# How q is turned for batches 1 to 7, and how a build-time planner chooses its next operation

## The chip, the cores and the metric

The kernel runs on one core of a Trainium2 chip, all of it in float32. The metric is the device time of one execution in microseconds, shown as the median of three runs. A profile is one execution recorded by the hardware profiler. The engines are called as in the profile: PE (TensorE), with PEld for its weight loads, DVE (VectorE), ACT (ScalarE), POOL (GpSimd) and SP (SyncE, which issues most DMAs here).

## The reference, cut to what matters

```python
# q, k, v: (8 batches, 8 heads, 576 rows, 64); w1: (4, 512, 1024); w2: (4, 1024, 512)
kv = np.einsum('bhsd,bhse->bhde', k, v)
out = np.einsum('bhsd,bhde->bhse', q, kv)
rms = np.sqrt(np.mean(out * out, axis=-1, keepdims=True) + 1e-06)
attn = out / rms * g_norm
x = attn.transpose(0, 2, 1, 3).reshape(4608, 512)
p = domain_probs / (domain_probs.sum(-1, keepdims=True) + 1e-09)
for e in range(4):
    h = np.maximum(x @ w1[e], 0.0)
    out_moe += p[:, e:e + 1] * (h @ w2[e])
```

A linear attention without softmax, each head's row scaled by the root of its mean square, and then four experts whose outputs are summed with weights.

## The kernel before

**Work and steps.** The 4608 rows of x are cut into nine chunks of 512: chunk b (0 to 7) holds 512 rows of batch b, and chunk 8 the 64 rows that each batch leaves over. There are 36 steps, s = 9e + c, each one expert e on one chunk c. A step has an `up` part (x @ w1, ReLU) and a `down` part (h @ w2); both replace some products by sums of blocks (seven products in place of eight, in two layers: `up`, `down_deep`; one layer in `down`). Step 0 is plain in `up_plain`. Attention for chunk c + 1 is done inside step c of expert 0, so steps 0 to 6 carry the attention of batches 1 to 7. Batch 0 is done ahead of all, in `opening`.

**The planner.** The order is not that of the code. Each piece of work is entered in a `Plan` as an operation with a key (its wanted place, in steps), a cost for each engine that may do it, the buffers it reads and writes, and further predecessors (`after`). `Plan.layout` (L91) then plays the operations through at build time and writes down one order for every engine; an engine may take an operation at most `REACH` keys beyond its first waiting one (L53). Buffers come from pools: `big`, `small`, `xf`, `q`, `kv` and others in SBUF, and eight PSUM banks in four kinds, two each: `u1` and `u2` (for `up`), `db` (for `down`), `ab` (for attention and some of `down_deep`). On the chip every engine goes through its list strictly in order, and waits by semaphores.

Three marks steer the choice: `early` keeps spare buffers free ahead of time, `gang` (on `attend`) reserves the banks of an operation that needs several at once, and `opens` holds back an operation that would take such a bank. In `down`, a list `firsts` and the list `second` add `after` edges between the first products of its two halves.

**Attention of batches 1 to 7** (`attention`, L888), for two groups s of two head pairs each:
- q's 576 rows of four heads arrive in 16 DMAs a batch, in runs of 32 numbers, so that halves of q's 64 dimensions lie on blocks of 32 partitions; DVE's transpose of 32 x 32 blocks (L975) then turns q in place.
- `key_values` (L996, matmuls at L1001): forty 64-column matmuls sum k'v for the two pairs into one `ab` bank; ACT copies the result.
- `attend` (L1021): 32 matmuls for the 512 rows into two `ab` banks (L1028), and 4 for the remaining 64 rows into two `db` banks (L1037).
- `evacuate` (L906): ACT or DVE copies the four results to SBUF, over q's own buffer.
- `norm_rows` (L914): ACT squares (L927), DVE sums (L933), POOL raises to the power -1/2 (L940, L944), DVE multiplies (L950).
- `turn_x` (L1066, L1069): eight 128 x 128 transposes on PE into two `ab` banks, and ACT writes them as chunk b's x with the gain (L1078).
- once a batch, `turn_left` (L1088): two transposes for the remainder, stored to a DRAM tile `x_left` (L1104).

**Attention of batch 0** (`opening`, L677) has another path: q's rows are loaded whole, PE turns q in `turn` (L742), ACT copies it; `attend` (L788) handles one pair at a time; `scaled` (L625) squares from PSUM (L640), sums (L647), raises to the power (L654, L658), and multiplies straight from PSUM (L667); `turn_x` (L806) does four transposes; the 64 remaining rows go through `turn_rem` (L832), `attend_rem` (L850), and `turn_xrem` (L866).

All products of the experts, and only they, run through the helper `halves_of` (L406, the matmuls at L410): each 128-column product is two matmuls of 64 columns.

Of the kernel before, what the change touches and what calls it, by code (L numbers as in the profile page):

```python
# [25 lines left out]
class Op:  # L26
    def __init__(self, key, cost, fn, reads, writes, kb, port):
        self.key, self.cost, self.fn, self.kb, self.port = key, cost, fn, kb, port
        self.outs = list(writes)
        self.bufs = list(dict.fromkeys(list(reads) + self.outs))  # L30
        self.deps = {}
        self.start = self.end = self.eng = None
        self.marks = self.seed = None
        self.early = self.gang = self.opens = False


BANKED = ("u1", "u2", "db", "ab")


class Plan:  # L40
# [12 lines left out]
    REACH = {"PE": 1.1, "DVE": 0.9, "ACT": 0.9, "POOL": 0.9, "SP": 1.0}  # L53
# [10 lines left out]
    def add(self, key, cost, fn, reads=(), writes=(), parts=(), kb=0, after=(), port=False, holds=(),  # L64
            early=False, gang=False):
# [3 lines left out]
        op.early, op.gang = early, gang  # L69
# [21 lines left out]
    def layout(self, slots, later, idle, idle_banks, idle_until):  # L91
# [60 lines left out]
        t = 0.0  # L152
# [4 lines left out]
        def ready(op, eng):  # L157
# [10 lines left out]
            for k, n in need.items():  # L168
                spare = self.SPARE.get(k, 0) if k != "xf" or op.key < self.FORMS else 0
                ahead = op.key > front + 0.1 and (eng == "SP" or op.early)  # L170
                if len(free[k]) < n + (spare if ahead else 0):
                    return None
# [11 lines left out]
        while left:  # L184
# [4 lines left out]
            for eng in todo:  # L189
# [9 lines left out]
                kept = {}  # L199
                for op in pending:  # L200
# [6 lines left out]
                    if op.opens and any(b.kind in kept for b in op.outs):  # L207
                        continue
                    when = ready(op, eng)
                    if when is None:  # L210
                        if op.gang and all(d.start is not None and d.end < t for d in op.deps):
                            kept.update((b.kind, True) for b in op.outs if b.kind in BANKED)
                        continue
                    if when > t:
                        if op.gang and all(d.end < t for d in op.deps):
                            kept.update((b.kind, True) for b in op.outs if b.kind in BANKED)
                        heapq.heappush(wake, when)
                        continue
# [77 lines left out]
def kernel(  # L296
# [76 lines left out]
    for kind, n in BANKS.items():  # L373
# [8 lines left out]
    QW = S * D // 32  # L382
    small_home = pool.tile([P, 4 * 2 * NT], F32, tag="small", name="small")
    kv_flat = kv_home[:].rearrange("p n x -> p (n x)")
    slots["kv"] = [kv_flat[:, i * KV:(i + 1) * KV] for i in range(4)]
    slots["kvbd"] = [kv_flat[:, 4 * KV + i * P:4 * KV + (i + 1) * P] for i in range(4)]
    slots["q"] = [small_home[:, i * QW:(i + 1) * QW] for i in range(2)]
    slots["small"] = [small_home[:, 2 * QW + i * NT:2 * QW + (i + 1) * NT] for i in range(3)]
# [3 lines left out]
        (("small", "q"), "w2y", [small_home[:, 2 * i * NT:2 * (i + 1) * NT] for i in range(2)]),  # L392
        (("small", "q"), "big", [small_home[:, 2 * i * NT:2 * (i + 1) * NT] for i in range(2, 4)]),
# [52 lines left out]
    def norm_probs(key):  # L446
        by_batch = moe_domain_probs.rearrange("(b s) e -> s b e", s=S)

        def load_all(eng):
            nc.sync.dma_start(  # L450
                out=p_all[:, 0:NR, :],
                in_=moe_domain_probs[0:NT, :].rearrange("(p r) e -> p r e", r=NR),
            )
            for r in range(NR):
                nc.sync.dma_start(  # L455
                    out=p_all[:, NR + r:B * NR:NR, :], in_=by_batch[r * P:(r + 1) * P, 1:, :])
# [15 lines left out]
        plan.add(key, {"SP": 4.0}, load_all, writes=[probs], kb=72)  # L472
# [204 lines left out]
    def opening(key, span, rem):  # L677

        b = 0
# [9 lines left out]
        splits = ((96, 6, 0),)  # L689

        def load_pair(hp):
            hs = slice(2 * hp, 2 * hp + 2)
            n = f"{b}_{hp}"
            kt, vt, qt = Buf("big", f"k{n}"), Buf("big", f"v{n}"), Buf("big", f"q{n}")
            want = key - 1 + 0.1 * hp
            load(
                want, qt, lambda qt=qt: qt.ap[:, 0:NT].rearrange("p (h x) -> p h x", h=2),
                q[b, hs, 0:NT, :].rearrange("h (p r) d -> p h (r d)", r=NR), 172,
            )
            for t, src in ((kt, k), (vt, v)):  # L700
                at_ = 0
                for rows, n_, size in splits:
                    load(
# [4 lines left out]
                        241,  # L708
# [15 lines left out]
        groups = ((0,), (1,), (2,), (3,))  # L724
        for g, pairs in enumerate(groups):
# [4 lines left out]
            for o, hp in enumerate(pairs):  # L730
# [4 lines left out]
                qT = qTs[hp] = Buf("big", f"qT{b}_{hp}")  # L735

                def turn(eng, bank=bank, qt=qt):
                    for r in range(NR):
                        rs = slice(r * P, (r + 1) * P)
                        for o in range(2):  # L740
# [7 lines left out]
                    at(hp), {"PE": 0.82}, turn, reads=[qt], writes=[bank])  # L748
# [3 lines left out]
                        out=qT.ap[:, 0:NT], in_=bank.ap[:], func=ACT.Copy),  # L752
# [3 lines left out]
            def key_values(eng, bank=kbank, held=held):  # L756
# [12 lines left out]
                at(pairs[-1]), {"PE": 0.73 * size + 0.2}, key_values,  # L769
# [8 lines left out]
            kind = ("db", "u2", "u1", "db")[g]  # L778
# [21 lines left out]
            for o, hp in enumerate(pairs):  # L800
                bank = Buf("ab", f"xT{b}_{hp}")

                def turn_x(eng, bank=bank, x=x, o=o):
# [13 lines left out]
                    reads=[bank, gains], parts=[xh],  # L817
# [4 lines left out]
        qr = Buf("big", f"qr{b}")  # L822
        load(
            at(1), qr, lambda: qr.ap[0:REM, 0:NT].rearrange("p (h d) -> p h d", d=D),
# [3 lines left out]
        qTr = Buf("big", f"qT{n}")  # L828
# [14 lines left out]
        rawr = [Buf("db", f"raw{n}_{r}") for r in range(2)]  # L843
# [16 lines left out]
        xr = Buf("big", f"x{n}")  # L860
# [3 lines left out]
        def turn_xrem(eng):  # L864
            for cc in range(NPAIR):
# [12 lines left out]
            reads=[xb], writes=[xs],  # L878
        )
        plan.add(  # L880
            at(NPAIR + 1) + 0.1, SPC,
            lambda eng: nc.sync.dma_start(
                out=x_left[:, :, b * REM:(b + 1) * REM],
                in_=xs.ap[:].rearrange("p (k t) -> p k t", k=4)),
            reads=[xs], writes=[left[b]], kb=128,
        )

    def attention(b, key, span, rem):  # L888

        at = lambda j: key + span * j / (NPAIR + 1)  # L890
        R = 32
        G = P // R
        splits = ((120, 4, 0), (96, 1, 480))

        def rows_of(t):

            at_ = 0
            for rows, n_, _ in splits:
                for j in range(n_):
                    yield [  # L900
                        t.ap[0:rows, at_ + (h * n_ + j) * D:at_ + (h * n_ + j + 1) * D]
                        for h in range(2)
                    ]
                at_ += 2 * n_ * D

        def evacuate(key, bank, src, to, dst, n):  # L906
            plan.add(
                key, {"ACT": 0.155 + 0.00088 * n, "DVE": 0.155 + 0.00104 * n},
                lambda eng: nc.vector.tensor_copy(out=dst(), in_=src()) if eng == "DVE"
                else nc.scalar.activation(out=dst(), in_=src(), func=ACT.Copy),  # L910
                reads=[bank], parts=[to],
            )

        def norm_rows(key, name, x, squares, count):  # L914

            ss, rt = Buf("ss", f"ss{name}"), Buf("rt", f"rt{name}")
            width = count * D

            def by_head(ap):
                return ap.rearrange("p (b d) -> p b d", d=D)  # L920

            for at_ in range(0, width, NT):
                n = min(width, NT)
                sq = squares or Buf("ab", f"sq{name}_{at_}")
                plan.add(
                    key, act(n),
                    lambda eng, sq=sq, at_=at_, n=n: nc.scalar.activation(  # L927
                        out=sq.ap[:, 0:n], in_=x.ap[:, at_:at_ + n], func=ACT.Square),
                    reads=[x], writes=[sq],
                )  # L930
                plan.add(
                    key, dve(n),
                    lambda eng, sq=sq, at_=at_, n=n: nc.vector.reduce_sum(  # L933
                        out=ss.ap[:, at_ // D:(at_ + n) // D], in_=by_head(sq.ap[:, 0:n]),
                        axis=AX.X),
                    reads=[sq], parts=[ss],
                )

            def power(eng):
                nc.gpsimd.tensor_scalar(  # L940
                    out=ss.ap[:, 0:count], in0=ss.ap[:, 0:count], scalar1=1.0 / D, scalar2=EPS,
                    op0=ALU.mult, op1=ALU.add,
                )
                nc.gpsimd.tensor_tensor(  # L944
                    out=rt.ap[:, 0:count], in0=ss.ap[:, 0:count], in1=mhalf[:, 0:count], op=ALU.pow)

            plan.add(key - 0.3, {"POOL": 0.3 + 0.19 * count}, power, reads=[ss], writes=[ss, rt])
            plan.add(
                key, dve(width),
                lambda eng: nc.vector.tensor_tensor(  # L950
                    out=by_head(x.ap[:, 0:width]), in0=by_head(x.ap[:, 0:width]),
                    in1=rt.ap[:, 0:count].unsqueeze(2).to_broadcast([P, count, D]), op=ALU.mult,
                ),
                reads=[x, rt], writes=[x], port=True,
            )

        xr, xs = Buf("snap", f"x{b}_r"), Buf("snap", f"xs{b}")
        for s in range(2):
            n = f"{b}_{s}"
            when = at(2 * s)  # L960
            qt = Buf("q", f"q{n}")
# [801 lines left out]
```

## Time and profile before

| what | us |
|---|---|
| median of 3 runs (lowest, highest) | 1665.1 (1664.63, 1666.04) |
| the profiled execution's own time | 1666.04 |
| its span, first to last instruction | 1664.0 |
| DVE busy | 1250.9 |
| ACT busy | 972.7 |
| POOL busy | 705.1 |

The span lies inside the time of its own execution, which was the slowest of the three. Busy time of PE is the union of matmuls, each taken from its start to a modelled end; the start of one matmul to the start of the next is the finer measure. The granted TensorE clock is 0.999 of full speed. The first 450 us are the steps of expert 0; the attention groups of batches 1 to 7 (L1001 to L1090) run from 38 to 378 us.

### The profile page before, as it was taken

How to read it: one execution, taken by the hardware profiler on the slowest of the kernel's cores; microseconds unless marked ns; L12 is line 12 of the kernel's file. 1: busy time of each engine (PE TensorE's matmuls, PEld its weight loads, DVE VectorE, ACT ScalarE, POOL GpSimd, SP SyncE). 2: the span in 40 equal slices, each digit the busy share in tenths (PEclk: the TensorE clock that was granted, in tenths of full speed). 3: DMA queues.
4: the chain of work that ended last, by engine and by line, in shares of the span. 5: the costliest groups of instructions: out<-in, count | busy, mean ns of one | idle time of the engine just before them, and what ended most of it. 6: DMA issues, size and time to landing. Idle time of an engine off the chain costs nothing.

```text
span 1664.0 us, 66253 instructions
## 1 busy us (share of the span) xinstructions
PE 1651.2 (99%) x28884; PEld 1557.9 (94%) x28884; DVE 1250.9 (75%) x2051; ACT 972.7 (58%) x2391; POOL 705.1 (42%) x701
## 2 busy tenths in 40 slices
PE   9999999999999999999999999999999999999998
PEld 6587888888899999999999999999999999999996
DVE  4768777677788877776778777777788778777774
ACT  2355555554456666666666665656566566666662
POOL 2545443343445343433354554333355555333321
PEclk9999999999999999999999999999999999999999
DMA  9776755535466454444577444444578444444443
GB/s 219 190 230 188 215 177 145 147 123 182 148 172 148 126 120 115 113 113 111 141 179 178 116 117 115 109 110 116 132 178 201 116 116 116 104 115 116 116 104 52
DMA packets 208123, 234.27 MB, mean 141 GB/s; under 512 B 97368, under 2 KB 148440, under 8 KB 207832
## 3 DMA queue, kind: packets, MB, share of 16 engines
q1 hardware_dynamic: 184760, 193.32, 38.4%
q0 software_dynamic: 23072, 36.71, 15.2%
q8 instruction: 227, 3.72, 0.9%
q14 instruction: 64, 0.52, 0.1%
HBM read 155.79 MB, written 74.19 MB: 138 GB/s over the span
## 4 chain that ended last, share of the span: by engine, by line
PE 96%; DMA 1%; POOL 1%; DVE 1%; SPq 1%; issue 0%; ACT 0%; DVEq 0%; POOLq 0%; ACTq 0%
PE u L410 46%; PE db L410 32%; PE ab L410 15%; PE ab L1001 1%; PE ab L1069 1%; DMA big<-in_v_dram 1%; PE ab L1028 1%; POOL rt L944 1%; DMA big<-in_moe_w_dram 0%; SPq L439 0%; POOL big L433 0%; DVE big L433 0%; SPq L455 0%; POOL ss L940 0%; PE ab L1090 0%
## 5 line engine op out<-in xcount | busy, mean ns | idle before, releaser
L433 DVE TENSOR_TENSOR big<-big,big 128x1024 f32<-128x1024 f32 (+1 forms) x527 | 518.8, 1001 | 34.1 <-ACT big L1226 15.9
L410 PE MATMUL u<-xf,big 128*64 128x128 f32 x6784 | 486.9, 273 | 0.2
L410 PEld LDWEIGHTS u<-xf,big 128*64 128x64 f32 x6784 | 393.9, 137 | 5.4 <-issue 1.0
L410 PE MATMUL u<-xf,w1y 128*64 128x128 f32 x5304 | 385.8, 273 | 0.0
L410 PE MATMUL db<-big,big 128*64 128x128 f32 (+1 forms) x4280 | 359.7, 307 | 1.3 <-ACT big L1576 0.4
L1270 DVE TENSOR_TENSOR big<-u,snap 128x256 f32<-128x256 f32 x476 | 199.5, 421 | 209.1 <-PE u L410 136.4
L433 POOL TENSOR_TENSOR big<-big,big 128x256 f32<-128x256 f32 (+1 forms) x196 | 219.1, 1134 | 222.9 <-DVE big L433 118.4
L410 PEld LDWEIGHTS u<-xf,w1y 128*64 128x64 f32 x5304 | 308.9, 137 | 2.4 <-issue 1.0
L1262 ACT ACTIVATE snap<-u 128x256 f32<-128x256 f32 x490 | 188.3, 384 | 195.2 <-PE u L410 141.7
L410 PEld LDWEIGHTS db<-big,big 128*64 128x64 f32 x4280 | 261.7, 137 | 41.7 <-issue 2.6
L1262 ACT ACTIVATE big<-u 128x256 f32<-128x256 f32 x476 | 181.6, 384 | 66.2 <-PE u L410 41.4
L1576 ACT ACTIVATE snap<-db 128x256 f32<-128x256 f32 (+1 forms) x230 | 82.4, 358 | 116.5 <-PE db L410 105.9
L1226 ACT ACTIVATE big<-big 128x1024 f32<-128x1024 f32 x134 | 140.7, 1050 | 5.6 <-DVE big L433 3.7
L433 POOL TENSOR_TENSOR big<-big 128x512 f32<-128x512 f32 (+1 forms) x76 | 94.5, 1250 | 114.8 <-DVE big L433 82.0
L410 PE MATMUL db<-small,big 128*64 128x128 f32 (+1 forms) x1552 | 116.9, 274 | 0.0
L1429 POOL DMA_DIRECT2D out_dram<-big x108 | 94.4, 1004 | 50.1 <-ACT big L1406 47.8
L1584 DVE TENSOR_TENSOR big<-ab,snap 128x256 f32<-128x256 f32 x166 | 69.8, 421 | 56.1 <-ACT snap L1576 30.1
L1262 ACT ACTIVATE u<-u 128x256 f32<-128x256 f32 x245 | 91.1, 372 | 24.6 <-PE u L410 9.1
L433 DVE TENSOR_TENSOR big<-big 128x512 f32<-128x512 f32 (+1 forms) x131 | 101.1, 783 | 2.4 <-PE u L410 2.3
L1614 POOL TENSOR_TENSOR big<-big 128x512 f32<-128x512 f32 x21 | 26.8, 1276 | 173.6 <-DVE big L433 140.9
L1406 ACT ACTIVATE big<-big,p_all 128x256 f32<-128x256 f32 x200 | 94.5, 501 | 5.4 <-POOL big L1614 4.0
L410 PEld LDWEIGHTS db<-small,big 128*64 128x64 f32 x1552 | 91.3, 137 | 0.7
(193 smaller groups left out, 2339.8 us busy)
## 6 DMA issues: line engine op xcount, KB each, us to landing
xf<-x SPq DMA_DIRECT2D x108, 512.0 KB, 3.6
out_dram<-big POOLq DMA_DIRECT2D x92, 256.0 KB, 5.5
xf<-x_h SPq DMA_DIRECT2D x81, 256.0 KB, 3.2
xf<-x SPq DMA_DIRECT2D x81, 256.0 KB, 3.6
x<-xf SPq DMA_DIRECT2D x36, 512.0 KB, 4.3
big<-in_moe_w_dram SPq DMA_DIRECT2D x32, 512.0 KB, 5.1
x_h<-big SPq DMA_DIRECT2D x18, 512.0 KB, 3.6
out_dram<-big SPq DMA_DIRECT2D x32, 256.0 KB, 3.5
```

Of the source, the lines that this page charges most:

```text
L410: nc.tensor.matmul(out_[cols], lhsT=lhsT[:, cols], rhs=rhs, **kw)
L433: lambda eng: adder(eng).tensor_tensor(out=out_(), in0=a(), in1=b(), op=op),
L944: nc.gpsimd.tensor_tensor(out=rt.ap[:, 0:count], in0=ss.ap[:, 0:count], in1=mhalf[:, 0:count], op=ALU.pow)
L1001: nc.tensor.matmul(bank.ap[r * D:(r + 1) * D, o * D:(o + 1) * D], lhsT=ks[r], rhs=vs[r], start=(j == 0), stop=(j == len(sets) - 1), skip_g ...
L1226: lambda eng: nc.scalar.activation(out=b.ap[:], in_=b.ap[:], func=ACT.Relu),
L1262: lambda eng: nc.scalar.activation(out=where(), in_=ps.ap[:, 0:HN], func=ACT.Copy),
L1270: lambda eng: nc.vector.tensor_tensor(out=block(whole, a, t), in0=src.ap[:, 0:HN], in1=add_.ap[:], op=ALU.add),
L1406: lambda eng: nc.scalar.activation(out=cell(i, half), in_=ap(), func=ACT.Copy, scale=prob()),
L1429: nc.gpsimd.dma_start(out=dst, in_=cell(i)[parts, :], accum_op=ALU.add)
L1576: lambda eng: nc.scalar.activation(out=where(), in_=group_of(ps.ap), func=ACT.Copy),
L1584: lambda eng: nc.vector.tensor_tensor(out=cell(tq, dq), in0=group_of(src.ap), in1=group_of(add_.ap), op=ALU.add,),
L1614: lambda eng: adder(eng).tensor_tensor(out=whole(to), in0=whole(a), in1=whole(b), op=ALU.add),
```

## The change

The attention of batches 1 to 7 goes back into the function that does batch 0, which is now called `attention(b, ...)` for every b. In it, for b of at least 1:
- q comes as whole rows of 64 numbers, 8 DMAs for the 512 rows of a batch and one for the remainder, into `small` buffers (eight of 512 columns in place of three, and no `q` buffers);
- PE turns q by four 128 x 128 transposes for each head pair; ACT copies each result;
- `key_values` and `attend` handle two pairs; the results are squared and multiplied straight from PSUM, in `ab` banks (`db` for batch 1);
- `turn_x` does four transposes at a time; the remainder has its own `turn_rem`, `attend_rem` and `turn_xrem`.

The former `attention` with `evacuate` and `norm_rows` is gone. The planner loses `early`, `gang` and `opens`; PE's reach is 0.7 in place of 1.1; `firsts` is gone and `second` is kept within one `down`; one form of x has key 0.80 in place of 0.60. The probabilities come in three DMAs in place of seven, and a partition of the output store of chunks 1 to 7 holds rows p·4 + i in place of i·128 + p.

```diff
-    REACH = {"PE": 1.1, "DVE": 0.9, "ACT": 0.9, "POOL": 0.9, "SP": 1.0}
+    REACH = {"PE": 0.7, "DVE": 0.9, "ACT": 0.9, "POOL": 0.9, "SP": 1.0}
...
-                ahead = op.key > front + 0.1 and (eng == "SP" or op.early)
-                if len(free[k]) < n + (spare if ahead else 0):
+                if len(free[k]) < n + (spare if eng == "SP" and op.key > front + 0.1 else 0):
...
-                    if op.opens and any(b.kind in kept for b in op.outs):
-                        continue
...
-    slots["q"] = [small_home[:, i * QW:(i + 1) * QW] for i in range(2)]
-    slots["small"] = [small_home[:, 2 * QW + i * NT:2 * QW + (i + 1) * NT] for i in range(3)]
+    slots["small"] = [small_flat[:, i * NT:(i + 1) * NT] for i in range(8)]
...
-    def opening(key, span, rem):
-        b = 0
+    def attention(b, key, span, rem):
...
+                for r in range(2):
+                    load(
+                        want, qt,
+                        lambda qt=qt, r=r: qt.ap[:].rearrange(
+                            "p (r h d) -> p r h d", h=2, d=D)[:, :, r, :],
+                        q[b, 2 * hp + r, 0:NT, :].rearrange("(p r) d -> p r d", r=NR), 128,
+                    )
...
-        groups = ((0,), (1,), (2,), (3,))
+        groups = ((0,), (1,), (2,), (3,)) if b == 0 else ((0, 1), (2, 3))
...
                     for r in range(NR):
                         rs = slice(r * P, (r + 1) * P)
+                        if b:
+                            nc.tensor.transpose(bank.ap[:, rs], qt.ap[:, rs], ident[:])
+                            continue
...
-            kind = ("db", "u2", "u1", "db")[g]
+            kind = ("db", "u2", "u1", "db")[g] if b == 0 else "ab" if b > 1 else "db"
...
-                    after=(second[-1:] if m in (1, 5) else []) + firsts[t:t + 1],
+                    after=second[-1:] if t and m in (1, 5) else (),
...
-                    after=(inner_last[-2:-1] or primed) + (second[-1:] if mixed else []) if mm == 1 else seeds if mm == 5 else (),
+                    after=(inner_last[-2:-1] or primed) if mm == 1 else seeds if mm == 5 else (),
```

## The prediction

> **What bounds the kernel now.** I read the page's busy table and its chain of waits first. Columns: engine, busy us, share of the span, instructions; then shares of the chain.
>
> ```profile
> PE 1651.2 (99%) x28884; PEld 1557.9 (94%) x28884; DVE 1250.9 (75%) x2051; ACT 972.7 (58%) x2391; POOL 705.1 (42%) x701
> ...
> PE 96%; DMA 1%; POOL 1%; DVE 1%; SPq 1%; issue 0%; ACT 0%; DVEq 0%; POOLq 0%; ACTq 0%
> ```
>
> TensorE (PE) sets the end: 1664.0 - 1651.2 = 12.8 us of the span are free of a matmul, 4.4 of them after the last one. The granted clock is 0.999, so no time hides there. Every us added to PE's own work lengthens the kernel by a us; work taken from DVE, ACT, POOL or the queues gives back at most what PE waits for it. The table of PE's waits (engine, line, waited-for; total, times, longest) says how much that is in the part that changes:
>
> ```profile
> PE ab L1069 <- DVE ss L933: 1.6, 1, 1.6
> PE ab L1090 <- DVE snap L950: 1.0, 1, 1.0
> ```
>
> With 0.8 us more at L1069, PE waits 3.4 us for attention's chains of batches 1 to 7. That is all that lighter side engines could give back.
>
> **What PE pays for a group of instructions.** "Busy" overlaps (a matmul's 273 ns is its latency), so I price by starts: from a group's first start to the next group's in the timeline of PE alone (start, us, line, tiles, shape, count). Four stretches: the new path's pieces do not occur in batches 1 to 7, but the opening (batch 0) has each of them.
>
> ```profile
> 269.34 1.09 PE L1069 MATMUL ab<-ident,small 128*128 128x128 f32 x8
> 270.37 0.66 PE L410 MATMUL u<-xf,big 128*64 128x128 f32 x8
> 270.85 0.61 PE L410 MATMUL u<-xf,w1y 128*64 128x128 f32 x8
> 271.29 0.61 PE L410 MATMUL u<-xf,big 128*64 128x128 f32 x8
> 271.83 0.44 PE L1090 MATMUL ab<-ident,snap 128*128 128x128 f32 x2
> 272.19 1.95 PE L410 MATMUL db<-big,big 128*64 128x256 f32 x16
> ...
> 288.24 0.61 PE L410 MATMUL u<-small,w1y 128*64 128x128 f32 x8
> 288.78 1.16 PE L1028 MATMUL ab<-kv,small 64*64 64x64 f32 x64
> 289.76 0.40 PE L1037 MATMUL db<-kv,small 64*64 64x64 f32 x8
> 290.09 0.66 PE L410 MATMUL u<-small,big 128*64 128x128 f32 x8
> ...
> 26.64 0.66 PE L806 MATMUL ab<-ident,big 128*128 128x128 f32 x4
> 27.23 1.94 PE L410 MATMUL u<-big,big 128*64 128x512 f32 x8
> ...
> 41.84 0.68 PE L850 MATMUL db<-kv,big 64*64 64x64 f32 x16
> 42.45 1.08 PE L410 MATMUL u<-big,big 128*64 128x512 f32 x4
> ...
> 52.65 0.46 PE L866 MATMUL ab<-ident,big 64*128 64x64 f32 x4
> 53.03 1.51 PE L410 MATMUL u<-big,big 128*64 128x512 f32 x6
> ```
>
> A product of eight takes 271.29 - 270.85 = 0.44 before another product, but 271.83 - 271.29 = 0.54 before a transpose, and the same 0.54 before an attend. So each such group costs a lead of 0.10 besides its own starts. With the lead: eight transposes 270.37 - 269.34 + 0.10 = 1.13; two (`turn_left`) 0.46; an attend with its remainder (L1028, L1037) 290.09 - 288.78 + 0.10 = 1.41; four transposes (L806) 0.59 + 0.10 = 0.69; four small ones (L866) 0.48; an `attend_rem` (L850) 0.71. An attend without its remainder: its 0.98, plus some 0.11 that the following remainder now hides of its end, plus the lead: 1.19 (estimate).
>
> **The change, part by part.**
>
> *Attention of batches 1 to 7* is the main term. Before, one batch needs two attends, two groups of eight and one `turn_left`: 2 x 1.41 + 2 x 1.13 + 0.46 = 5.54 us of PE. After, q is turned on PE: four `turn` of four transposes (2.76), two attends without remainder (2.38), four `turn_x` of four (2.76), and the remainder's `turn_rem`, `attend_rem`, `turn_xrem` (0.48 + 0.71 + 0.48): 9.57. `key_values` is the same forty matmuls twice. The difference is 4.03 a batch, 28.2 in seven. In the changed program's order 19 of these groups stand right behind another transposing group, and such a join saves: eight in one group cost 1.13, two fours 1.38, so 0.25. At 0.21 on the mean (ten joins are with small groups, of which before shows none) that is 4.0 off: **+24.2 us**. Bounds: with everything joined, four transposes cost half of 1.03 and no lead is paid: 2.06 + 2.38 + 2.06 + 0.38 + 0.61 + 0.38 = 7.87, less 5.54, times 7 = +16.3; with no join, +28.2. I take 24.2, as the order's joins are counted.
>
> The built programs agree on the count: 14,704 matmuls of the source against 14,550, 154 more: per batch 16 for q, 8 for the remainder, less 2 for `turn_left`.
>
> The Trainium skill, in "VectorE: DVE Perf Modes", section "The three transpose paths", gives a full 128x128 transpose on TensorE as 390 ns (bf16), and in "Rules for kernel authors" names TensorE as the engine for it. By its figure the 154 would cost 60 us (estimate), and the time would be some 1725; the rows above, 1.03 us for eight in place, decide against that figure. Its advice doesn't ask which engine is full: here VectorE has a quarter of the span free and TensorE nothing.
>
> *What the side engines lose and gain.* DVE drops two StreamTransposes (1.37 each, L975), and its copies out of PSUM; ACT gains four copies of q (0.60 each, the row of L910) and drops its evacuations. Both are idle a quarter or more of every such stretch and hide it; without that cover it would be some 1 us a batch. I cost both at nothing beyond the waits.
>
> *The wait that is added.* `turn_x` waits for square, sum, power and multiply, as before, but the attend's two PSUM banks are now held until the multiply, and the same two banks serve q's turns. Behind a late `turn_x` stand products of the expert, which wait with it. The opening has the same chain at half size (last group: attend issued until 22.33, turned from 26.64: 4.3 us):
>
> ```profile
> 22.45 0.66 ACT L640 ACTIVATE big<-db 128x256 f32<-128x256 f32 x2 [1.43 <-PE db L788]
> 23.14 0.69 DVE L647 TENSOR_REDUCE ss<-big 128x8 f32<-128x512 f32 x1 [2.29 <-ACT big L640]
> 24.20 1.64 POOL L658 TENSOR_TENSOR rt<-ss,mhalf 128x8 f32<-128x8 f32 x1
> 25.87 0.76 DVE L667 TENSOR_TENSOR big<-db,rt 128x256 f32<-128x256 f32 x2 [1.38 <-POOL rt L658]
> ```
>
> At double size: 0.1 + 1.1 (ACT) + 1.3 (sum) + 0.4 + 2.9 (the power at 16 columns, median of L944) + 1.4 (two multiplies) = 7.2 us. The changed order, priced with the rows above, leaves 8.1 us of PE work for it once (batch 1), 9.3 to 10.2 in the first group of batches 2 to 7, 11 to 20 in the second; the remainder's chain (about 4.3) has 6.2 to 7.4. Before, a chain of about 9.7 (289.8 to the multiply's end at 299.4) had about 11 and PE did not wait; where it had 7.9, PE lost 0.9. Margins stay near 2 us, so I put the waits after equal to before's 3.4, a net of 0. Bounds: -3.4 if all vanish; +10.5 if each of 21 chains (three a batch) is 0.5 late.
>
> *The planner* (PE's reach 1.1 to 0.7 keys, `gang`, `opens` and `firsts` gone, other `after` edges, key 0.8 for one form of x) only reorders. In experts 1 to 3 the two PE orders have the same shortest distances from a product through ACT or DVE to the next product that needs it (0.9 to 1.8 us), and PE's idle time from 1000 to 1600 us is 0.05: nothing. The opening's PE order is the same up to the first q of batch 1. The last stretch keeps its thirteen `down` products, then a multiply-add and a store: the 4.4 us tail stays.
>
> *SP's queue.* A batch's q comes in 8 DMAs of 128 KB plus one remainder in place of 16 of 72 KB; the probabilities in 3 DMAs in place of 7, of which four took 4.21 us to issue (L455). Everything behind them, k and v, w2 and the stores, moves forward; the first turn of q is needed at about 30 us, and its two loads stand eighteenth in the queue, where before the first q stood. No gain is booked, since PE waited only 0.2 us for a DMA; the cost, if q came late, is in the bounds of the waits. Stores' rows change place, not their size.
>
> **Sum.** 1664.0 + 24.2 + 0 = 1688.2 span of the profiled execution, which itself took 1666.04, 0.94 over the median of 1665.1. Set on the median: 1665.1 + 24.2 = **1689.3 us**, +1.5%.
>
> **The rivals.**
> - *Late chains.* The two `ab` banks make q's turns wait for multiplies, and each wait delays what follows. For it: the banks are held 7 us longer three times a batch. Against: the margins. At 0.5 to 1 us for 21 chains: 1700 to 1710. Chance 0.14.
> - *Cheap groups.* More joins than I count and PE's 3.4 us gone: 1665.1 + 16.3 - 3.4 = 1678 to 1684. For it: lighter DVE and queues. Against: leads and ends repeat to 0.01 us wherever the trace has them. Chance 0.11.
> - *Hidden slack, not slower.* In expert 0 PE issues fewer matmuls than later; if that were slack, the new groups would fall into it:
>
> ```profile
> 350.00:400.00 50.00, 50.00 (x766) 42.53 (x764) 35.69 (x64) 27.48 (x63) 16.62 (x17) 1.00 0.31 107
> ```
>
>   Against 916 per 50 us from 500 to 1000, 766 is 16% less; 8% over some 300 us would be 24 us, the whole cost, from which point the 3.4 us decide: 1662 to 1665. But the rows speak against it: 128-wide products follow at 0.44 there too, and the rest are 256-wide ones that take twice as long. Chance 0.03.
> - *It does not do what it says*: the counted 154 matmuls exclude that.
>
> **How the numbers follow.** My case, 1684 to 1696, has 0.72. The range for 8 in 10 reaches into late chains and cheap groups: 1681 to 1701. About 0.2% (3.3 us) is what a measurement of this kernel tells from no change; all cases but slack lie above 1668.4. Faster 0.02, same 0.01, slower 0.97.
>
> **What would show it.** Matmul records up by about 154 (a transpose leaves one record); q's turns at 0.59 to 0.69 from start to start, and `turn_left` gone; PE's free time still 10 to 16 us; expert 0 longer by 24 us and experts 1 to 3 as long as before. I am wrong if PE's idle time in the first 450 us grows beyond 5 us, if the new groups cost under 0.5 us each, or if the later steps change by more than 2 us.

## The result, and the profile after

| | before | after |
|---|---|---|
| median of 4 runs, side by side, us | 1665.3 | 1685.87 |
| lowest and highest | 1664.63, 1666.04 | 1685.14, 1687.89 |
| span of the profiled execution | 1664.0 | 1683.6 |
| its own time | 1666.04 | 1685.35 |

The ratio is 1.0125, 95% interval [1.0108, 1.0143]: slower by 20.6 us, where 24.2 were predicted. The spans differ by 19.6 (the profiled execution before was the slowest of its four, that of the changed kernel among the faster); I explain that difference, since both profiles belong to it.

The page of the changed kernel, its busy times and its chain of waits:

```profile
PE 1675.1 (99%) x29038; PEld 1571.4 (93%) x29038; DVE 1217.8 (72%) x2050; ACT 979.9 (58%) x2405; POOL 703.6 (42%) x667
...
PE 99%; issue 0%; ACT 0%; POOL 0%; DVE 0%; POOLq 0%; ACTq 0%
```

PE has 29038 matmuls in place of 28884, the 154 that were counted. Its busy time grew by 23.9 us, while the time without any matmul fell from 12.8 to 1683.6 - 1675.1 = 8.5. DVE has 33 us less to do, and no saving of that size appears: the chain is PE's to 99%.

The table of PE's waits after (engine, line, waited-for; total, times, longest), all that it names:

```profile
PE ab L1479 <- POOL ident masks.py:199: 1.4, 1, 1.4
PE ab L755 <- issue: 1.0, 1, 1.0
PE ab L1479 <- issue: 0.4, 1, 0.4
PE ab L860 <- ACT big L808: 0.3, 1, 0.3
PE ab L736 <- ACT kv L768: 0.3, 1, 0.3
```

The waits of batches 1 and 2 for a chain through DVE, which stood here before (1.6, 1.0, 0.8), are gone. One of 0.3 for ACT (L860, the remainder's turn) is all that attention of batches 1 to 7 still has.

The new groups, in PE's own timeline (start, us, line, tiles, shape, count; L732 turns q, L800 turns x, L860 the remainder's x, L395 is a product):

```profile
286.73 0.66 PE L800 MATMUL ab<-ident,big 128*128 128x128 f32 x4
287.31 0.46 PE L860 MATMUL ab<-ident,small 64*128 64x64 f32 x4
287.70 0.66 PE L395 MATMUL u<-xf,w1y 128*64 128x128 f32 x8
288.19 0.61 PE L395 MATMUL u<-xf,big 128*64 128x128 f32 x8
288.73 0.66 PE L800 MATMUL ab<-ident,big 128*128 128x128 f32 x4
289.22 0.60 PE L732 MATMUL ab<-ident,small 128*128 128x128 f32 x4
289.75 1.09 PE L395 MATMUL db<-w2y,big 128*64 128x128 f32 x16
...
293.83 0.66 PE L732 MATMUL ab<-ident,small 128*128 128x128 f32 x4
294.42 0.66 PE L395 MATMUL u<-small,w1y 128*64 128x128 f32 x8
```

A single turn of q takes 294.42 - 293.83 = 0.59 from start to start, and 288.73 - 288.19 = 0.54 shows the lead of 0.10 on the product ahead of a turning group. The pair at 288.73 is a join: two fours in 289.75 - 288.73 = 1.02 with one lead, 1.12, against 2 x 0.69 = 1.38 apart. The product behind a group is slower too: 288.19 - 287.70 = 0.49 in place of 0.44.

The stretch of experts 1 to 3 (columns: stretch, us, then busy time and count of PE, PEld, DVE, ACT, POOL, clock, DMA share, GB/s), in the kernel before:

```profile
1000.00:1600.00 600.00, 599.95 (x10992) 599.71 (x10990) 459.49 (x734) 375.77 (x947) 261.00 (x254) 1.00 0.51 125
```

and in the changed kernel:

```profile
1000.00:1600.00 600.00, 599.95 (x10992) 599.71 (x10990) 459.75 (x732) 375.60 (x946) 264.68 (x256) 1.00 0.51 126
```

The same work at the same rate and the same clock: the planner's new order changed nothing there.

**Where the 19.6 us are.** I went through PE's matmuls from start to start. What a start lies later than the usual distance of its kind (by more than 20 ns) is a wait; the rest belongs to its group, and a lead to the group behind it. Sums in us, waits by where they fall (opening up to 25 us, expert 0 up to 450, later, and the end from 1600):

| kernel | attention's groups | products | opening | expert 0 | later | end | after the last matmul's start |
|---|---|---|---|---|---|---|---|
| before | 80.4 | 1565.9 | 2.5 | 7.2 | 0.6 | 1.2 | 4.8 |
| after | 104.3 | 1565.9 | 2.2 | 4.2 | 0.6 | 0.0 | 5.1 |
| difference | **+23.9** | 0.0 | -0.3 | **-3.1** | 0.0 | -1.2 | +0.3 |

The sum is +19.6. This finer measure sees more waits than the table of waits, which lists the larger ones.

The split between groups and waits hangs on the rule by 1 to 2 us. Single gaps of over 0.15 us make up 5.1 of the 7.2 us of expert 0 before, but only 0.6 of the 4.2 after. The rest are pieces of 0.02 to 0.15 us. Most regular among them is the 0.05 us by which the product behind a group is slower, 25 times before and 57 times after. If these pieces are counted with the groups that cause them, the groups' difference is some +25.5 and that of the waits in expert 0 some -4.6.

### The profile page after: what moved, and what is told of

It is laid out like the page before. It is cut to its first block, busy times and chain, and to the rows that moved or that the text cites. A ratio compares the mean times of both kernels' runs of the same rounds, so it can differ in the third digit from the quotient of the medians.

```text
span 1683.6 us, 66427 instructions
## 1 busy us (share of the span) xinstructions
PE 1675.1 (99%) x29038; PEld 1571.4 (93%) x29038; DVE 1217.8 (72%) x2050; ACT 979.9 (58%) x2405; POOL 703.6 (42%) x667
## 4 chain that ended last, share of the span: by engine, by line
PE 99%; issue 0%; ACT 0%; POOL 0%; DVE 0%; POOLq 0%; ACTq 0%
PE u L395 47%; PE db L395 32%; PE ab L395 14%; PE ab L755 1%; PE ab L800 1%; PE ab L732 1%; PE ab L782 1%; PE ab L1479 1%; PE ab L844 0%; PE ab L736 0%; PE db L782 0%; PE ab L826 0%; PE ab L860 0%; PE u L782 0%; ACT big L1034 0%
## 5 line engine op out<-in xcount | busy, mean ns | idle before, releaser
L418 DVE TENSOR_TENSOR big<-big,big 128x1024 f32<-128x1024 f32 (+1 forms) x525 | 509.2, 986 | 51.1 <-ACT big L998 21.3
L395 PE MATMUL u<-xf,big 128*64 128x128 f32 x6784 | 486.5, 273 | 0.2
L395 PEld LDWEIGHTS u<-xf,big 128*64 128x64 f32 x6784 | 392.8, 137 | 5.7 <-issue 1.3
L395 PE MATMUL u<-xf,w1y 128*64 128x128 f32 x5304 | 386.7, 273 | 0.0
L1042 DVE TENSOR_TENSOR big<-u,snap 128x256 f32<-128x256 f32 x478 | 200.5, 421 | 250.6 <-PE u L395 153.5
L395 PE MATMUL db<-big,big 128*64 128x128 f32 (+1 forms) x4304 | 362.2, 307 | 0.0
L418 POOL TENSOR_TENSOR big<-big,big 128x256 f32<-128x256 f32 (+1 forms) x204 | 236.2, 1170 | 260.9 <-DVE big L418 124.2
L395 PEld LDWEIGHTS u<-xf,w1y 128*64 128x64 f32 x5304 | 308.9, 137 | 3.0 <-issue 0.5
L395 PEld LDWEIGHTS db<-big,big 128*64 128x64 f32 x4304 | 263.4, 137 | 39.3 <-issue 0.3
L395 PE MATMUL db<-small,big 128*64 128x128 f32 x1512 | 113.8, 274 | 0.0
L395 PE MATMUL ab<-big,big 128*64 128x128 f32 (+1 forms) x1328 | 93.4, 276 | 0.0
L1177 ACT ACTIVATE big<-big,p_all 128x256 f32<-128x256 f32 x186 | 88.0, 501 | 4.1 <-POOL big L1381 3.7
```

The costliest lines, as they stand in the source:

```text
L395: nc.tensor.matmul(out_[cols], lhsT=lhsT[:, cols], rhs=rhs, **kw)
L418: lambda eng: adder(eng).tensor_tensor(out=out_(), in0=a(), in1=b(), op=op),
L1042: lambda eng: nc.vector.tensor_tensor(out=block(whole, a, t), in0=src.ap[:, 0:HN], in1=add_.ap[:], op=ALU.add),
L1177: lambda eng: nc.scalar.activation(out=cell(i, half), in_=ap(), func=ACT.Copy, scale=prob()),
```

## Experiments

Ratios are to the kernel before, run on the same chip with each of them. The changed kernel was run in its own series only; before's median lay between 1665.3 and 1666.5 us in the series, so a difference to the changed kernel is good to about 1 us. "Groups" and "waits" are the columns of the table above for the run's own profile, by the same rule.

### e1: q turned twice (result unchanged)

```diff
-                            nc.tensor.transpose(bank.ap[:, rs], qt.ap[:, rs], ident[:])
+                            for _ in range(2):
+                                nc.tensor.transpose(bank.ap[:, rs], qt.ap[:, rs], ident[:])
```

> The changed kernel, with every 128x128 transpose of q for batches 1 to 7 done twice into the same place (the result is unchanged): 112 more transposes, inside their groups. Theory (a transpose costs its start-to-start time in a group, 0.109 us, and lead and end of the group are paid once): +12.2 us, 1698. Rival 1 (the whole price of a group, 0.69 / 4 = 0.17 us, is each transpose's own): +19, 1705. Rival 2 (PE's new transposes lie in slack): under +4, 1686 to 1690. By the 390 ns of the Trainium skill's page VectorE: DVE Perf Modes it would be +44.

Measured 1697.84 us, ratio 1.0188 [1.0173, 1.0204], 12.0 above the changed kernel. Groups rose to 116.7 (+12.4), waits in expert 0 stayed at 4.2. So a transpose added to a group costs PE its 0.11 us, and all of it reaches the end: there is no slack under attention's groups.

### e2: turns of q and of x in pieces of eight

```diff
...
+                    def turn(eng, turned=turned):
+                        for bank, qt, _ in turned:
+                            for r in range(NR):
+                                rs = slice(r * P, (r + 1) * P)
+                                nc.tensor.transpose(bank.ap[:, rs], qt.ap[:, rs], ident[:])
...
+            plan.add(when, pe(4 * size, P, 1), turn_x, reads=[x], writes=xbanks)
...
```

> The changed kernel, with the q turns of a group's two pairs in one piece of eight transposes, and the same for x: no transpose more or less, but 28 pieces in place of 56. Theory (a piece that follows a product pays 0.10 lead and some 0.15 at its end): 15 fewer entries from a product into a transpose, and the joins that the changed kernel already has are lost: -3 to -4.5 us, 1681.5 to 1683, unless new waits for two free banks take it back. Rival (leads and ends are no cost of the switch): 0, 1686.

Measured 1682.43 us, ratio 1.0097 [1.0083, 1.011], 3.4 below the changed kernel; groups 100.7 (-3.6). A joined turn of q in PE's timeline of this run:

```profile
266.81 1.09 PE L750 MATMUL ab<-ident,small 128*128 128x128 f32 x8
267.83 0.44 PE L395 MATMUL u<-xf,w1y 128*64 128x128 f32 x4
```

Eight take 267.83 - 266.81 = 1.02, near the 1.03 of `turn_x` before. So fewer entries into transposes do save; the change could have been 3.4 us cheaper, but not cheap.

### e3 and e4: the probabilities' DMAs exchanged

Before with the three DMAs of the changed kernel, and the changed kernel with the seven of before.

```diff
...
-            for r in range(NR):
-                nc.sync.dma_start(
-                    out=p_all[:, NR + r:B * NR:NR, :], in_=by_batch[r * P:(r + 1) * P, 1:, :])
+                out=p_all[:, 0:B * NR, :].rearrange("p (b r) e -> p b (r e)", r=NR),
+                in_=by_batch[0:NT].rearrange("(p r) b e -> p b (r e)", r=NR),
...
```

> The kernel before with the probabilities loaded by three DMAs as in the changed kernel, all planned orders as before (each row then gets another row's probabilities). Theory A (before's PE waits at 62 to 73 us come from SP's queue: seven DMAs of probabilities hold back k, v and w2, and w2's sums then meet attention's chain on DVE and POOL): the waits there shrink from 3.4 to under 1.5 us, 1662 to 1663.5. Theory B (they come from attention's longer chain, evacuation first, against its place in PE's order): 3 to 4 us of waits stay, 1665.

> The changed kernel with the probabilities loaded by seven DMAs as in the kernel before, all planned orders unchanged (each row then gets another row's probabilities). Theory A (SP's queue): PE's waits between 40 and 80 us grow from some 0.6 to 2 us or more, 1687.5 to 1689. Theory B (the chain's length decides): unchanged, 1685.5 to 1686.5.

e3: 1664.8 us, ratio 0.999 [0.9981, 0.9998]; the wait at batch 1's first `turn_x` fell from 1.6 to 0.6, the other two stayed at 1.0 and 0.8, waits in expert 0 from 7.2 to 6.2. The second half of expert 0's w2 was issued at 45.3 us in place of 48.7. e4: 1685.89 us, ratio 1.0117 [1.0103, 1.013], no change, waits in expert 0 at 4.2. The fewer DMAs of the probabilities are worth 1 us of waits to the kernel before and nothing to the changed one. SyncE's issue of that half, in before, the changed kernel and e4:

```profile
48.70 0.99 SPq L439 DMA_DIRECT2D big<-in_moe_w_dram  x2
37.04 2.23 SPq L424 DMA_DIRECT2D big<-in_moe_w_dram  x2
40.42 1.15 SPq L424 DMA_DIRECT2D big<-in_moe_w_dram  x2
```

In before it stands behind the eight loads of k and v for batch 1's second group, in the other two ahead of them. With seven DMAs it still goes out at 40.4, so the probabilities account for 3.4 of the 11.7 us by which it is earlier; the rest is its place ahead of those loads and the shorter list of q's loads.

### e5: before, with later keys for the waiting turns

```diff
-            when = at(2 * s + 2.2)
+            when = at(2 * s + 2.2 + {1: 0.5, 2: 0.5}.get(b, 0.0) * (1 if b == 1 else s))
...
-        plan.add(at(NPAIR + 1), {"PE": 0.41}, turn_left, reads=[xr], writes=[xb])
+        plan.add(at(NPAIR + 1) + (0.1 if b == 1 else 0.0), {"PE": 0.41}, turn_left, reads=[xr], writes=[xb])
```

> The kernel before with later keys for turn_x of batches 1 and 2 and for turn_left of batch 1: in PE's order more products stand between attend and the transposes (second group of batch 2: 9.7 us in place of 7.9; remainder of batch 1: 12.7 in place of 10.3; the first group of batch 1 stays at 11.5). Theory (a wait is the chain's length less its distance in PE's order): the waits of 1.0 and 0.8 us go, the one of 1.6 stays; 1.5 to 2 us off the kernel before. Rival (the chain moves back with its transpose, since its engines are the bound there): no change, within 0.5 us.

A miss: 1668.49 us, ratio 1.0015 [1.0006, 1.0024], slower. The waits of 1.0 and 0.8 went, but the planner laid out everything behind them anew, and PE waited at products in their place: 8.0 in expert 0 and 2.6 later (0.6 before). A late turn could be moved, but not alone.

### e6: before, with PE's reach of the changed kernel

```diff
-    REACH = {"PE": 1.1, "DVE": 0.9, "ACT": 0.9, "POOL": 0.9, "SP": 1.0}
+    REACH = {"PE": 0.7, "DVE": 0.9, "ACT": 0.9, "POOL": 0.9, "SP": 1.0}
```

> The kernel before with PE's reach at 0.7 keys, the one planner edit of the change that this kernel's planner can take alone. It moves attention of batch 1 in PE's order: distances from attend to turn_x 9.7 and 7.9 us in place of 11.5 and 12.8, to turn_left 6.7 in place of 10.3. Theory (distance against a chain of 11 to 13 us in this stretch): waits grow from 3.4 to 5 to 8 us, 1.5 to 5 us slower than before. Rival (the shorter reach is what took the waits out of the changed kernel): waits shrink, 1 to 3 us faster than before.

1671.11 us, ratio 1.0034 [1.0022, 1.0047]; waits in expert 0 rose from 7.2 to 11.2, one of 5.1 at batch 1's first `turn_x`, and the later ones from 0.6 to some 4.6. So the shorter reach is not what removed waits. (The changed kernel built with a reach of 1.1 has the same order on every engine as with 0.7.)

### e7 and e8: the changed kernel, with q turned by DVE again

The changed attention and planner, but q loaded as halves on 32 partitions, turned by DVE, and the remainder's q with it; the probabilities by seven DMAs and the rows of the output store in the order of before. e8 also turns x in pieces of eight, as e2 does.

```diff
...
+                if b:
+                    plan.add(
+                        at(hp) - 0.1, dve(S),
+                        lambda eng, qt=qt: nc.vector.transpose(
+                            out=qt.ap[:, 0:S], in_=qt.ap[:, 0:S]),
+                        reads=[qt], writes=[qt],
+                    )
+                    qTs[hp] = qt
+                    continue
...
```

> The changed kernel with one part undone: q of batches 1 to 7 is again loaded in halves of its dimensions on 32 partitions and turned by DVE, the 64 remaining rows with it; attend, squares and multiplies from PSUM, four transposes a piece for x, and a remainder of its own stay as changed (with the row order and the probabilities' seven DMAs that this q needs). PE loses 28 turns of q and 7 turn_rem. Theory (price by groups): 2 x 1.19 + 4 x 0.69 + 0.71 + 0.48 = 6.33 us a batch against 5.54 before, less 11 joins (2.3 in all): +3.2 us on before, less 0 to 3 us of waits: 1665 to 1669, so 17 to 21 us off the changed kernel. Rival (half of the loss or more lies in the other parts: x in pieces of four, the separate remainder, the planner): 1672 or more.

> The former kernel with x's transposes in pieces of eight: 2 x 1.19 + 2 x 1.13 + 0.71 + 0.48 = 5.83 us a batch against 5.54, some 0.8 less for joins: +1.2 us on before, less 0 to 3.4 us of waits, 1662.5 to 1666.5. Theory: 1 to 3 us faster than the former kernel, and no slower than before by more than 1. Rival (holding two ab banks at once for x brings the waits back): as slow as the former kernel or slower.

e7: 1672.31 us, ratio 1.0037 [1.0024, 1.0049]; groups 83.0, so turning q on PE is 104.3 - 83.0 = 21.3 of the 23.9 us. The groups came as expected (83.0 - 80.4 = +2.6; +3.2 was counted), but the waits and the time did not: 12.9 in expert 0. By its time alone, over 1672, the run would speak for the rival; but 6.3 us of the 20.6 are left against before, not half, and by the table's columns most of them are waits. e8 missed as well: 1671.64 us, ratio 1.0037 [1.0025, 1.005]; groups 81.6, waits 10.5 in expert 0 and 3.2 later. Neither beats the kernel before. In both, the waits at the end are 0.0, as in the changed kernel. As both have q and the rows of the stores as before, those 1.2 us came with neither; the planner's new order is what is left, and no run shows it alone.

PE's longest wait in e7, from the table of waits:

```profile
PE db L395 <- DVE big L652: 4.0, 1, 4.0
```

That is a product that needs the banks that batch 1's second multiply (L652) frees, 71 us into the span. Ahead of that multiply stood sums over w2's blocks, whose second half was issued at 50.2 us here, 48.7 in before and 37.0 in the changed kernel. That suggested the next two runs.

### e9 and e10: only w2 moved, to and fro

The planned order of every engine is kept but for SyncE: in before, the two loads of w2's second half are put right behind those of the first; in the changed kernel, as late as their readers allow, and one of them three times over.

```diff
+    loads = {b.name: o for o in order if o.eng == "SP" for b in o.outs}
+    moved = [loads[n] for n in ('w2_0_12', 'w2_0_3')]
+    order = [o for o in order if o not in moved]
+    at = order.index(loads["w2_0_2"]) + 1
+    order[at:at] = moved
```

> The kernel before with one thing moved: SyncE issues the two loads of the second half of expert 0's w2 right behind those of the first half (36 to 37 us) and not behind the probabilities and eight loads of k and v (48.7 us). Nothing else changes place on any engine. Theory (the waits of before come from late w2: its two 128x1024 sums on GpSimd, 2.35 us each, stand ahead of the power of batch 1's first group, and GpSimd stood idle until 54.9 us for that transfer): the wait at the first turn of x of batch 1 (62 us, 1.6) goes to under 0.5, GpSimd's first such sum starts at 45 to 49 us in place of 54.9, the kernel is 1 to 3 us faster (1662.3 to 1664.3). Rival 1 (the chain's own length decides, square, evacuation, sum, power, multiply): the 1.6 us stay, and the time is that of before within 0.4 us. Rival 2 (what is moved back, probabilities and k and v, is late in its turn): the wait goes, others come at the key_values of batch 1's second group, and it is slower by 0.5 to 2 us.

> The changed kernel with the same two loads the other way: SyncE issues them behind seven of the eight loads of k and v of batch 1's second half, and the first of the two three times over (the same 512 KB into the same buffer), so that they land some 10 us later, at about 54 us as in the kernel before. The order on every other engine is unchanged. Theory (when w2 lands decides the waits): GpSimd's sum of w2 and DVE's two stand ahead of the power and the sum of squares of batch 1's first group, the multiply comes 4 to 10 us later, and PE waits 3 to 9 us more in expert 0: 1689 to 1695. Rival (the shorter chain without evacuation, or the longer list of PE work, hides it): under 1 us more, 1685.5 to 1687.

e10: 1696.7 us, ratio 1.0184 [1.017, 1.0198], 10.8 above the changed kernel, somewhat more than the 3 to 9 expected. Waits in expert 0 rose from 4.2 to 13.3. GpSimd's first sum over that half, in the changed kernel and in e10 (in brackets: idle before, and for whom):

```profile
43.48 2.36 POOL L418 TENSOR_TENSOR big<-big,big 128x1024 f32<-128x1024 f32 x1
54.44 2.34 POOL L418 TENSOR_TENSOR big<-big,big 128x1024 f32<-128x1024 f32 x1 [10.22 <-DMA big<-in_moe_w_dram]
```

and PE's table of waits in e10:

```profile
PE db L786 <- DVE big L653: 5.2, 1, 5.2
PE ab L759 <- DMA kv<-in_v_dram: 1.8, 1, 1.8
```

GpSimd stood 10 us idle for w2, the power of batch 1's first group, next in its list, came that much later, and the second `attend` (L786) waited for the multiply. The 1.8 are k and v, late behind the repeated loads. So with the changed order, the early landing of w2 is a condition of the few waits.

e9 is the reverse, and it missed: 1666.7 us, ratio 1.0003 [0.9994, 1.0012]. The wait at batch 1's first `turn_x` fell from 1.6 to 0.6, as in e3, but waits in expert 0 only from 7.2 to 6.3. GpSimd's sum over w2's second half, in before and in e9:

```profile
54.93 2.38 POOL L433 TENSOR_TENSOR big<-big,big 128x1024 f32<-128x1024 f32 x1 [7.77 <-DMA big<-in_moe_w_dram]
56.80 2.36 POOL L433 TENSOR_TENSOR big<-big,big 128x1024 f32<-128x1024 f32 x1 [6.81 <-DVE small L433]
```

These starts can't be compared as they stand. The profiled execution of e9 left the opening 2.8 us later than that of before: the first product of step 0 starts at 27.60 in place of 24.77, and the longest wait ahead of it is 2.8 in place of 1.5. DVE's sum over the probabilities (L464) is later by just that, 50.73 in place of 47.93, and in neither did DVE wait for them. Against the rest of the kernel, GpSimd's sum came 1.0 us earlier, which is what the wait of PE lost. Then, by the profile, it waited for a sum of DVE's (56.26 to 56.67), where it had waited for w2 before. So the expected 45 to 49 us was out of reach for an early w2 alone; the next thing it needed came only 1 us before w2 did. The 1.0 us doesn't show in the time of the runs, 0.35 above before.

### e11 and e12: the hybrid of e8 with w2 early, and with its sums moved

e11 is e8 with the move of e9. e12 also changes three places in the order:

```diff
...
+    behind([at("DVE", f"w2_0_{n}")[0] for n in (5, 6, 7, 4)], at("DVE", "xg1_0")[1])
+    behind(at("POOL", "h5_0")[:1], at("POOL", "ss1_1")[0])
+    behind(at("DVE", "h6_0")[:1] + at("DVE", "h3_0")[:1], at("DVE", "xg1_1")[1])
```

> The kernel of the run e8 (q turned by VectorE, x in pieces of eight) with one thing moved: the two loads of the second half of expert 0's w2 are issued right behind the first half (37 us in place of 50). Theory (late w2 holds up batch 1's chain): VectorE no longer waits for that transfer (1.06 us at 56.8), the sum of squares of the second group starts 1 to 2 us earlier than 60.6, and PE's waits in expert 0 fall from 10.5 by 1 to 3: 1668.5 to 1670.7. Rival (only the place of w2's four sums in VectorE's order, between the square and its sum, costs): the same within 0.7 us, 1671 to 1672.3.

> The same, and three places changed in the order of VectorE and GpSimd: w2's four sums of 128x1024 stand behind the multiply of batch 1's first group and no longer between the squares of the second group and their sum; the power of the second group stands ahead of the 128x1024 sum of the hidden values on GpSimd (2.36 us), and VectorE's two sums of hidden values stand behind the multiply. Theory (the waits of e7 and e8 are a matter of the order around batch 1's second chain): its multiply, at 69.6 us in e8, comes 3 to 4 us earlier, PE's waits in expert 0 fall to 4 to 7 us, 1665.5 to 1668.5, level with the kernel before or a little slower. Rival (the chain's length itself is too much for this PE order): the wait at the first product of w2 (2.8) stays over 2 us, and the time over 1669.5.

Both missed. e11: 1673.19 us, ratio 1.0041 [1.0028, 1.0055], waits in expert 0 at 10.3 (e8: 10.5). e12: 1672.72 us, ratio 1.0035 [1.0022, 1.0047], waits 10.6; the wait at the first product of w2 fell from 2.8 to 1.1, and others came. Behind expert 0 both wait another 3 to 4 us, as e8 does. DVE's timeline in e12 shows where the largest comes from:

```profile
49.95 0.30 DVE L449 TENSOR_REDUCE tot<-p_all 128x36 f32<-128x144 f32 x1 [4.18 <-DMA kv<-in_v_dram]
```

PE's longest wait in e12:

```profile
PE ab L816 <- DVE big L652: 2.6, 1, 2.6
```

DVE stood 4.2 us ahead of the probabilities' sum. The profile puts that down to a DMA of v; the instruction itself reads the probabilities, whose last DMA was issued at 47.6 us (44.9 in e8), behind w2 and after a slower issue of four of them (7.4 us; 5.4 in e8). Behind that sum stood the multiply (52.5 to 53.7) for which the first `turn_x` (L816) waits 2.6. A load moved forward pushes another one back, and DVE, in its fixed order, waited for the later one.

## Why the prediction was right, point by point

**Attention's groups, +24.2.** Measured +23.9 by the rule of the table, some +25.5 when the small pieces are counted with the groups. The price of four transposes (0.69 with lead), of an `attend` alone (1.19), of the remainder's pieces, and 19 joins at 0.21 hold together to 0.3 us by the first, to 1.3 by the second. What the price left out is the slower product behind a group, which its own rows show (270.85 - 270.37 = 0.48 against 0.44): 32 more of them are 1.6 us. e1 and e2 measure two parts singly: 0.11 us for a transpose added to a group, 3.4 us for the groups joined. The figure of 390 ns (bf16) in the Trainium skill ("VectorE: DVE Perf Modes", section "The three transpose paths"), which the prediction set aside, would have made e1 slower by 44 us (estimate); it was slower by 12.0. The case *hidden slack* fell with e1 too: all of the added work arrived.

**Waits, net 0.** This is the term that was mis-sized: it measured -4.6 (some -6.1 if the small pieces are left to the groups), below the lower bound of -3.4, since that bound took only the three waits that the table names. So the total came 3.6 us under the forecast, by a gain that the prediction had not foreseen. Of it, -0.3 in the opening is no effect (the twelve other profiles have 1.4 to 3.6 there). -1.2 at the end goes, by e7 and e8, neither with q nor with the stores; the planner's order is what is left. In expert 0 there are two sources at least. The new order of SyncE's queue and its smaller list bring w2's second half 12 us earlier; with it late, waits come back and more (e10, +9.1, of which 1.8 are for k and v), while in the kernel before an earlier w2 alone removes 1.0 (e3, e9). The other 2 us or so by the table's rule (3.6 by gaps over 0.15 us), the late chains of batches 1 and 2 and products beside them, I could not pin down: a chain without evacuation is shorter (in the changed kernel a full group's squares start at 270.45 us and its power ends at 276.44, 6.0 us; in before it is 8.2 from the copies at 290.01 to 298.17), more work of PE lies beside it, and the planner's other edits move both, but no run separated them. That the chain alone doesn't do it, e7 shows: the same chain with 12.9 us of waits, and 10.3 in e11 with w2 early.

**The chain of 7.2 us and its margins.** No `turn_x` of batches 1 to 7 waits for it, so *late chains* fell; e10 shows at which price it would have come. The length itself was too short: in the group at 270 us the multiplies end at 279.45, 9.0 us after the squares start, as they begin 1.7 us after the power.

**Planner.** Experts 1 to 3 as long as before: right. That it "only reorders" was too mild for expert 0 and the end: e5 and e6, orders laid out anew with the same instructions, are slower by 2.5 and 5.1 us.

**SP's queue, at nothing.** Half right. The three DMAs of the probabilities are worth 1 us of waits in before (e3) and nothing in the changed kernel (e4). But w2's early place in the queue is needed there (e10). The reason given, that PE waited only 0.2 us for a DMA, missed that GpSimd waited 7.8 us for w2 in before, and that 1.0 of PE's 1.6 us at the first `turn_x` came from there (e9).

**What would show it.** 154 more records: right. Turns of q at 0.59: right, 0.49 to 0.53 in joins. PE's free time at 10 to 16 us: wrong, it is 8.5, by the waits above. Expert 0 longer by 24: it is 23.9 - 3.1 = 20.8. PE's idle time in the first 450 us fell, from 7.6 to 3.6, in place of growing.

## What to carry to other kernels

When one engine is busy to 99%, price an edit by what it adds to that engine from start to start, with the lead of a switch in kind of work; that sum held to about 1 us in 24 here, while of 33 us taken from VectorE no more than part of 5 to 6 us of waits can have come back. For the small rest, the waits, bound the gain by every gap of the limiting engine and not only by those that a table names. In a program whose order is planned as a whole, moving one load or one turn can move the waits elsewhere (e5, e12): look for what arrives next before you move it.

## What the hardware showed

A VectorE sum of two SBUF operands doesn't run beside a sum of 128x1024 on GpSimd. DVE's timeline in e11:

```profile
63.95 2.53 DVE L418 TENSOR_TENSOR big<-big 128x256 f32<-128x256 f32 x1
```

and GpSimd's at that time:

```profile
63.85 2.35 POOL L418 TENSOR_TENSOR big<-big,big 128x1024 f32<-128x1024 f32 x1 [0.42 <-ACT big L1139]
```

The DVE instruction takes 0.41 us elsewhere; here it ends 0.3 us after GpSimd's. In the trace of before, six such sums of 128x256 start inside a GpSimd sum, with a median of 1.64 us against 0.41 for 428 others, and in the changed kernel six, with 2.3 against 0.41. Narrower sums of GpSimd hold them up as well (thirteen inside 128x512 in before: median 1.06), its power doesn't (eight inside one of 128x16: 0.41). Sums of the same size with one operand in PSUM (L1270 before, L1042 after) keep their 0.42 us there, over twenty times in each. The Trainium skill says the same ("SBUF — State Buffer", section "SBUF: two separate sides"): the two engines share a pair of ports as a lock, which a VectorE instruction with two SBUF inputs needs. That GpSimd's power, which reads SBUF too, doesn't hold the sums up goes against the page, which makes no such exception. It enters no term of the prediction, but a chain through DVE can lose 2 us to it.

SyncE's four issues of the probabilities in runs of 16 bytes took 4.2 us in before, 5.9 in e7, 7.3 in e9 and 7.4 in e12, with the same shapes. What stretched them isn't shown.
